# One pass over the weights for token groups 0 and 1, a sign taken as a bit, and batch 0's q and k transposed by TensorE

## The chip, the core and the metric

One core of one Trainium2 chip runs the whole kernel. The metric is the device time of one execution in microseconds (us). The kernel before was timed three times: 1012.99, 1014.65 and 1016.63 us, median 1014.65 us.

## The reference

Three layers run one after another, on 2304 tokens (4 batches of 576) of width 512 (8 heads of 64):

```python
scores = scale * q @ k.T + (cum[:, None] - cum[None, :])   # cum = cumsum(log f); causal mask
x = softmax(scores) @ v                                    # (4, 8, 576, 64) -> (2304, 512)
g = x @ w_gate;  x = silu(g) * (x @ w_val) @ w_out         # 512 -> 1536 -> 512, weights as float64
e = argmax(x @ r_gate);  gw = 1 / (sum(exp(l - max l)) + 1e-9)
out = gw * relu(x @ w1[e]) @ w2[e]                         # 8 experts, 512 -> 1024 -> 512
```

All three are computed to nearly float32, mostly by splitting each operand into a high and a low half (`hi`, `lo`) and adding three products: hi·hi, hi·lo and lo·hi.

## The kernel before, in words

**Attention.** Two heads make a pair `P`; batch 0 is pairs 0 to 3, and a batch has 16 steps ("slots"). In slot i, `part1` scores one item (a head and a half of its query blocks; L279), `part2` (L340) casts and splits the probabilities of item i-1 and has them transposed by a DMA (L366, `pt<-p`), and `pv` (L371) multiplies item i-2 by the values. While pair P runs, pair P+1 is prepared: `scales` (L191) finds a power of two for q and k, and `prep` (L216) splits q and k of one head into f16 halves side by side on the 128 partitions (L230 and L235 on ACT, L234 on DVE) and has them transposed by a DMA (L237, `qkt<-qks`). A score block is then two matmuls (L262, L263), one for the decay (L265) and one for the mask (L270).

**Weights.** The weights of the second layer arrive as 64-bit floats. `decode` (L871) rebuilds a 128x512 float32 tile from one 512 KB load of word pairs (`lo`, `hi`): two ACT operations on the high word (L878 the magnitude, L879 the sign as +1 or -1), a shift on DVE (L880), a shift-and-or on DVE that brings in the low word (L881), and a multiplication by the sign on POOL (L884). `w_split` (L900) then makes f16 halves of the gate and value weights (L909 on ACT, L910 on DVE), and `wo_dec` (L912) splits an output weight tile. For each j of 6 (256 of the 1536 inner columns) there are nine such tasks: 4 decodes and 2 splits of gate and value weights, one small one, and 2 output-weight decodes; over all j 36 decodes. The list `tasks` (L923) holds them in order of j. The load buffers are one tile and four not-yet-used weight tiles of j = 4 and 5; from j = 3 on fewer of these are left.

**Second layer.** Tokens go in 9 groups `g` of 256; a unit u is one (g, j): `unit_g` (L521) and `unit_v` (L532) are 24 matmuls each (L503), and `unit_o` (L546) adds 12 matmuls (L556) into two PSUM tiles `yp`, which stay open over the six j of a group. `fin0` (L587) copies them out and writes the rows to DRAM (`y_d`). Units run in the order u = 6g + j (L522).

**Order of the work.** The code is written as a list with due points, and a planner then places each engine's instructions by that order and by when operands should be ready. Before unit 0 come the first 18 slots, all of batch 0, and with them 43 of the 57 tasks (`PRE`, L1148, L1160), that is all of j = 0 to 3 and most of j = 4. The rest follow at the units that need them (`mark`, `markw`, L1109, L1174). Slots of batch 1 start to be dealt out after unit 4 and are due at unit 10 (`pts_`, L1165); group 2, which begins batch 1's tokens, is unit 12.

**Third layer.** `fin1`, `fin2` (L608, L638) find each token's expert and its gate weight `gw`, write the latter to DRAM (`g_d`, L735), and list tokens by expert. Experts follow one by one; a last tile of overflowing tokens gathers its gate weights from `g_d` (L1366), and a loop (L1414) is there for more such tiles.

Of the kernel before, what the change touches and what calls it, by code (L numbers as in the profile page):

```python
# [12 lines left out]
U32 = mybir.dt.uint32  # L13
# [14 lines left out]
def kernel(  # L28
# [37 lines left out]
    g_d = dram.tile([NT + 1, 1], F32, name="g_d")  # L66
# [19 lines left out]
    cnt = const.tile([128, NE], F32, name="cnt")  # L86
    sv = const.tile([128, 2, B], F32, name="sv")
# [9 lines left out]
    def consts():  # L97
# [32 lines left out]
        vec.memset(cnt, 0.0)  # L130

# [24 lines left out]
    qk_in = [ap_.tile([128, 2, NCH, D], F32, name=f"qk_in{i}") for i in range(NQK)]  # L156
# [34 lines left out]
    def scales(P):  # L191
        am = st_p.tile([128, 2], F32, tag="am", bufs=2, name="am")
        jk = qks_p.tile([128, 3 * NCH, 2, D], F16, tag="qks", name="jk").rearrange("p (a c) h d -> p a c h d", a=3)
        for a in range(2):
            act.activation(
                out=jk[:, a].rearrange("p c h d -> p h c d"), in_=qk_in[(2 * P + a) % NQK], func=ACTF.Square,
                accum_out=am[:, a:a + 1],
            )
# [16 lines left out]

    def prep(P, hh):  # L216
        sc, c = stt[P]
# [20 lines left out]
        heads[P, hh] = (qkt, c[1][:, hh, :])  # L238
# [19 lines left out]
    def score(ps, o, hd, j, k0, k1):  # L258
        qkt, pk = hd
        n = k1 - k0  # L260
        lq = qkt[:, 0, 128 * j:128 * j + 128]
        pe.matmul(out=ps[:, o:o + n], lhsT=lq, rhs=qkt[:, 1, k0:k1], start=True, stop=False, skip_group_check=True)  # L262
        pe.matmul(out=ps[:, o:o + n], lhsT=lq, rhs=qkt[:, 2, k0:k1], start=False, stop=False, skip_group_check=True)  # L263
# [256 lines left out]

    def unit_g(u):  # L521
        g, j = divmod(u, KF // 2)  # L522
# [9 lines left out]
    def unit_v(u, t):  # L532
        g, j = divmod(u, KF // 2)
# [12 lines left out]
    def unit_o(u):  # L546
        g, j = divmod(u, KF // 2)
        hi, lo = hbuf.pop(u)
        if j == 0:
            yps[g] = [ps_y.tile([128, DM], F32, tag=f"y{i}", name="yp") for i in range(2)]  # L550
        for i in range(2):
            n_ = 0
            for fi in range(2):
                fk = 2 * j + fi
                for hx, wx in ((hi, 0), (hi, 1), (lo, 0)):
# [4 lines left out]
                        start=(j == 0 and n_ == 0),  # L560
                        stop=(j == KF // 2 - 1 and n_ == 5),
# [24 lines left out]

    def fin0(g):  # L587
        ys = M["y"].tile([128, 2, DM], F32, tag="ys", name="ys")
        act.activation(out=ys[:, 0, :], in_=yps[g][0], func=ACTF.Copy)
        vec.tensor_copy(out=ys[:, 1, :], in_=yps[g][1])  # L590
# [47 lines left out]
    def fin2(g):  # L638
# [96 lines left out]
        rows_out(g_d, g, gw)  # L735
# [37 lines left out]
    def start():  # L773
# [25 lines left out]
        act.dma_start(out=g_d[NT:NT + 1, :], in_=zr[:, 0:1])  # L799
# [71 lines left out]
    def decode(src, n):  # L871
        c = c_tile()
        raw = fetch(src, n, c.rearrange("p (a n) -> p a n", a=n))
        if raw is not None:
# [3 lines left out]
            act.activation(out=c, in_=hi.bitcast(F32), func=ACTF.Abs, scale=2.0 ** -112)  # L878
            act.activation(out=hi.bitcast(F32), in_=hi, func=ACTF.Sign)  # L879
# [4 lines left out]
            gp.tensor_tensor(out=c, in0=c, in1=hi.bitcast(F32), op=ALU.mult)  # L884
# [37 lines left out]
    NJ = KF // 2  # L922
# [179 lines left out]
    def unit(u, between=None):  # L1102
# [5 lines left out]
        if u > 0:  # L1108
            if u - 1 < NJ:  # L1109
                upto(markw[u - 1])  # L1110
            unit_o(u - 1)
            g1, j1 = divmod(u - 1, NJ)
# [10 lines left out]
            if j1 == NJ - 1:  # L1123
                if g1 == 0:
                    sg.close()
                    M.update(routing_pools())
# [21 lines left out]
    PRE0, PRE = 2, 43  # L1148
# [16 lines left out]
    pts_ = [(-1, first), (NJ - 2, first), (2 * NJ - 2, 8 * NP + 2), (4 * NJ - 1, 12 * NP + 2), (6 * NJ - 2, NSL)]  # L1165
# [7 lines left out]
    for u in range(NU + 1):  # L1173
        if u < NJ:  # L1174
            upto(mark[u])
        if u < NU and u % NJ == 0:
            for b, _, _ in spans(min(u // NJ + 1, NG - 1)):
# [4 lines left out]
        if u < NU:  # L1182
            need = 4 * NP * ((G * (u // NJ + 1) - 1) // S + 1) + 2
        tgt = pace(u)
        slots(need)
        unit(u, lambda: slots(min(tgt, nslot[0] + 1)))
# [162 lines left out]

    def gate(s, t):  # L1350
# [4 lines left out]
    for s in range(NE + 1):  # L1355
        nxt = s + 1 if s < NE else None
        if s == 2:
# [8 lines left out]
            gp.indirect_dma_start(  # L1366
                out=gwo, out_offset=None, in_=g_d[:, :],
                in_offset=bass.IndirectOffsetOnAxis(ap=ixo.bitcast(U32), axis=0),
            )
# [19 lines left out]
        if nxt is not None:  # L1389
            if nxt == 1:  # L1390
                transp(xts[1], 0, xgs[1], bank)
            else:
                turn(xts[nxt % 2], xgs[nxt])
        if nxt == NE:
# [16 lines left out]
    with tc.tile_pool(name="lw", bufs=1) as lw, tc.tile_pool(name="lr", bufs=3) as lr, tc.tile_pool(  # L1411
        name="lx", bufs=1
    ) as lx, tc.tile_pool(name="lp", bufs=2, space=PSUM) as lp:
        with tc.For_i(1, n_ov) as it:  # L1414
# [8 lines left out]
            gp.indirect_dma_start(  # L1423
# [56 lines left out]
```

## Time and profile before

| | |
|---|---|
| median of 3 runs | 1014.65 us |
| the profiled execution's own time | 1012.41 us |
| its span, first to last instruction | 1010.6 us |
| busy: TensorE (PE) | 882.2 us, 87% |
| busy: VectorE (DVE) | 614.9 us, 61% |
| busy: ScalarE (ACT) | 555.3 us, 55% |
| busy: GpSimd (POOL) | 389.6 us, 39% |
| mean granted TensorE clock | 0.943 |

The shares are means over stages that differ. The page cuts the span into 40 slices of 25.3 us: in the first six or seven PE is half idle while DVE and ACT are nearly full, and later PE is busy at 95% or more. "Releaser" in a wait is what ended an engine's idle time. Clock 1.00 is 2.4 GHz and 0.50 is 1.2 GHz.

### The profile page before, as it was taken

Reading aid. Unit: us, or ns where it says so; the run is one execution under the profiler, and the core shown is the slowest. Engines: PE = TensorE matmul, PEld = TensorE weight load, DVE = VectorE, ACT = ScalarE, POOL = GpSimd, SP = SyncE. Lnnn points to the kernel's source line nnn. Section 1 sums busy time; section 2 is a strip of 40 time slices with the busy share of each in tenths; the row PEclk is TensorE's granted clock in tenths of the full one; section 3 lists DMA queues with packets and bytes.
Section 4 is the critical chain, followed back from the end, with each engine's and each line's share of the span. In section 5 each row is a group of like instructions: output and inputs, shape, how many; then the busy total and the mean of one; then the engine's idle time right before and its main releaser. Section 6 shows DMA issues by size and latency. Waiting matters only on the chain.

```text
span 1010.6 us, 19838 instructions
## 1 busy us (share of the span) xinstructions
PE 882.2 (87%) x7028; PEld 734.7 (73%) x7053; DVE 614.9 (61%) x1818; ACT 555.3 (55%) x1205; POOL 389.6 (39%) x467
## 2 busy tenths in 40 slices
PE   1545557998999989999999999898989999999995
PEld 0334336877777868888878888687869788889894
DVE  6999888487666746565644434334536675665540
ACT  5987988476677666665633322122425454555431
POOL 1468676464444425344442222222245632100101
PEclk9995657999999999999999999899989999999998
DMA  8897998347886787567545422112376887765420
GB/s 244 209 216 205 230 204 187 90 101 165 180 172 146 164 190 158 101 133 137 102 113 143 121 22 64 5 18 66 71 180 187 218 219 201 215 198 159 132 95 34
DMA packets 309481, 146.35 MB, mean 145 GB/s; under 512 B 273441, under 2 KB 285857, under 8 KB 309380
## 3 DMA queue, kind: packets, MB, share of 16 engines
q1 hardware_dynamic: 305088, 134.68, 56.2%
q0 software_dynamic: 4096, 10.24, 3.7%
q8 instruction: 56, 0.92, 0.4%
q14 instruction: 45, 0.37, 0.2%
q10 hardware_dynamic: 196, 0.14, 0.0%
HBM read 84.24 MB, written 10.31 MB: 94 GB/s over the span
## 4 chain that ended last, share of the span: by engine, by line
PE 46%; DMA 17%; issue 12%; DVE 6%; ACT 3%; SPq 2%; POOL 2%; POOLq 0%; DVEq 0%; ACTq 0%
PE yp L556 11%; PE g L503 10%; PE v L503 10%; DMA out_dram<-o,ix 5%; PE bank L1218 3%; DMA pt<-p 3%; PE px L387 2%; DMA pair<-yt 2%; PE bank L1261 2%; DMA pair<-words 2%; DMA wr<-in_moe_w_dram 1%; PE ps L262 1%; PE ps L263 1%; DVE wlo L978 1%; PE ps L265 1%
## 5 line engine op out<-in xcount | busy, mean ns | idle before, releaser
L352 POOL TENSOR_TENSOR p<-st,p 128x128 f16<-128x128 f32 (+3 forms) x128 | 110.1, 864 | 102.1 <-issue 62.7
L543 POOL TENSOR_TENSOR lo<-t,hi 128x512 fp32r<-128x512 f32 x54 | 70.1, 1299 | 149.3 <-ACT hi L542 121.6
L503 PE MATMUL g<-xr,wga 128*128 128x256 f16 x864 | 106.1, 277 | 0.3 <-DVE t L529 0.3
L503 PE MATMUL v<-xr,wva 128*128 128x256 f16 x864 | 106.2, 277 | 0.0
L327 ACT ACTIVATE st<-st,nb,c 128x64 f32<-128x64 f32 (+4 forms) x160 | 102.6, 643 | 0.9
L503 PEld LDWEIGHTS <-wga 128*128 128x128 f16 x864 | 82.6, 100 | 17.2 <-issue 6.6
L503 PEld LDWEIGHTS <-wva 128*128 128x128 f16 x864 | 84.8, 101 | 10.6 <-issue 0.3
L387 PE MATMUL px<-vs,pt 128*128 128x64 f16 x1280 | 56.3, 203 | 39.3 <-DMA pt<-p 28.8
L349 DVE CAST p<-st 128x64 f16<-128x64 f32 (+4 forms) x160 | 68.4, 442 | 31.6 <-ACT st L327 20.1
L317 DVE CUSTOM_DVE_ANT_0 st<-ps,zero 128x64 f32<-128x64 f32 (+3 forms) x160 | 55.8, 377 | 50.9 <-PE ps L270 48.8
L387 PEld LDWEIGHTS <-pt 128*128 128x128 f16 x1280 | 50.3, 105 | 49.3 <-DMA pt<-p 32.8
L363 POOL TENSOR_TENSOR p<-st,p 128x64 f16<-128x64 f32 (+1 forms) x128 | 54.1, 424 | 70.6 <-issue 36.4
L262 PE MATMUL ps<-qkt 128*128 128x64 f16 (+2 forms) x192 | 56.5, 312 | 21.1 <-DMA qkt<-qks 7.2
L526 ACT ACTIVATE t<-g,gscale 128x512 f32<-128x512 f32 (+3 forms) x72 | 39.4, 573 | 62.2 <-PE g L503 59.0
L1012 POOL DMA_INDIRECT out_dram<-o,ix x24 | 24.6, 1026 | 123.3 <-ACT o L1263 79.5
L542 ACT ACTIVATE hi<-t 128x512 fp32r<-128x512 f32 x54 | 33.8, 625 | 56.5 <-DVE t L536 56.5
L556 PE MATMUL yp<-wohi,hi 128*128 128x512 f32 x144 | 60.6, 421 | 0.0
L263 PE MATMUL ps<-qkt 128*128 128x64 f16 (+2 forms) x192 | 60.1, 315 | 0.0
L1223 ACT ACTIVATE h<-bank 128x320 fp32r<-128x320 f32 (+1 forms) x64 | 26.3, 422 | 60.1 <-PE bank L1218 59.8
L1225 DVE SCALAR_TENSOR_TENSOR h<-bank,h 128x64 fp32r<-128x64 f32 (+2 forms) x128 | 33.4, 305 | 40.4 <-ACT h L1223 40.4
L556 PE MATMUL yp<-wohi,lo 128*128 128x512 f32 x144 | 57.6, 402 | 0.0
L556 PE MATMUL yp<-wolo,hi 128*128 128x512 f32 x144 | 57.1, 397 | 0.0
(322 smaller groups left out, 2483.2 us busy)
## 6 DMA issues: line engine op xcount, KB each, us to landing
wr<-in_moe_w_dram SPq DMA_DIRECT2D x72, 512.0 KB, 5.1
vr<-in_v_dram SPq DMA_DIRECT2D x16, 288.0 KB, 4.5
qk_in<-in_q_dram SPq DMA_DIRECT2D x32, 128.0 KB, 2.5
qk_in<-in_k_dram SPq DMA_DIRECT2D x32, 128.0 KB, 2.6
v_in<-in_v_dram SPq DMA_DIRECT2D x32, 128.0 KB, 3.0
y_d<-ys SPq DMA_DIRECT2D x6, 512.0 KB, 3.5
wgb<-in_moe_w_gate_dram SPq DMA_DIRECT2D x5, 512.0 KB, 5.9
raw<-in_moe_w_val_dram SPq DMA_DIRECT2D x5, 512.0 KB, 4.2
```

Of the source, the lines that this page charges most:

```text
L262: pe.matmul(out=ps[:, o:o + n], lhsT=lq, rhs=qkt[:, 1, k0:k1], start=True, stop=False, skip_group_check=True)
L263: pe.matmul(out=ps[:, o:o + n], lhsT=lq, rhs=qkt[:, 2, k0:k1], start=False, stop=False, skip_group_check=True)
L317: vec.tensor_tensor_reduce(out=sts[m][:, k0 - 64:k1 - 64], in0=ps[:, o:o + n], in1=zero.to_broadcast([128, n]), scale=1.0, scalar=init, op ...
L327: act.activation(out=sts[m], in_=sts[m], func=ACTF.Exp, scale=c[:, 0:1], bias=nb[:, m:m + 1], accum_out=sm[:, m, hh:hh + 1],)
L349: vec.tensor_copy(out=flat[:, o + 64:o + 64 + n], in_=src)
L352: gp.tensor_tensor(out=flat[:, o1:o1 + n - 64], in0=src[:, 64:n], in1=flat[:, o + 128:o + 64 + n], op=ALU.subtract)
L363: gp.tensor_tensor(out=blk[:, :, 0:64], in0=pair, in1=blk[:, :, 64:128], op=ALU.subtract)
L387: pe.matmul(out=px[:, 128 * m + 64 * hh:128 * m + 64 * hh + 64], lhsT=pm[:, o + ph * last + c, :], rhs=vs[:, hh, c, vh, :], start=(c == 0 ...
L503: pe.matmul(out=ps[:, fi, :], lhsT=w16[:, kk, wi, 128 * fi:128 * fi + 128], rhs=xr[:, kk, x0:x0 + 2, xi, :], start=(n_ == 0), stop=(n_ == ...
L526: act.activation(out=t[:, :, c0:c1], in_=gps[:, :, c0:c1], func=ACTF.Tanh, scale=gscale[:, b, j:j + 1])
L543: last["lo"] = gp.tensor_tensor(out=lo, in0=t, in1=hi.bitcast(F32), op=ALU.subtract)
L556: pe.matmul(out=yps[g][i], lhsT=hx[:, fi, 128 * i:128 * i + 128], rhs=wo[fk][wx], start=(j == 0 and n_ == 0), stop=(j == KF // 2 - 1 and n ...
```

## The change

- **Order.** Units run as (0,0) (0,1) (0,2), then group 1's six, then (0,3) (0,4) (0,5), then groups 2 to 8. So j = 3, 4, 5 are first needed at units 6, 7, 8. Group 0's half sum is copied out of PSUM and written to `y_d` (`part_out`), and `fin0(0)` reads it back and adds the second half.
- **Tasks.** 27 of the 57 (j = 0 to 2) are traced with batch 0's slots; the other 30 with units 0 to 4. Slots of batch 1 are dealt out from unit 0 on and are due at unit 10 as before.
- **Decode.** The magnitude keeps nothing of the sign; a second shift-and-or form on DVE takes the sign bit from the high word. L879 (ACT) and L884 (POOL) go.
- **Batch 0's q and k** (`prep0`): ten TensorE transposes of 128x128 per pair into PSUM, both heads at once; ACT and DVE then scale, split and write f16 halves, q once per head with the other head's rows multiplied by 0. A score block has three products instead of two. L230, L234, L235 and L237 are not run for these pairs; batches 1 to 3 keep them.
- **Gate weights** are no longer written to DRAM; the overflow tile computes its own (`gate_of`: 8 small matmuls and five short operations).

The core of the diff:

```diff
+    def prep0(P):
+        vec.tensor_scalar(out=qm, in0=half, scalar1=sc[:, 0, 0:1], scalar2=None, op0=ALU.mult)
...
+        for a in range(2):
+            src = qk_in[(2 * P + a) % NQK]
...
+            for x in range(NCH):
+                o = ps[:, 128 * x:128 * x + 128] if x < NCH - 1 else last_[:, 128 * a:128 * a + 128]
+                pe.transpose(out=o, in_=src[:, :, x, :], identity=ident)
...
+            for n0, n1, p in parts:
+                if a == 0:
+                    for h in range(2):
+                        act.activation(out=two[h][:, 0, n0:n1], in_=p, func=ACTF.Copy, scale=qm[:, h:h + 1])
+                        vec.scalar_tensor_tensor(
+                            out=two[h][:, 1, n0:n1], in0=p, scalar=qm[:, h:h + 1], in1=two[h][:, 0, n0:n1],
+                            op0=ALU.mult, op1=ALU.subtract,
+                        )
+                else:
+                    s1 = sc[:, 0, 1:2]
+                    act.activation(out=two[0][:, 2, n0:n1], in_=p, func=ACTF.Copy, scale=s1)
+                    vec.scalar_tensor_tensor(
+                        out=two[1][:, 2, n0:n1], in0=p, scalar=s1, in1=two[0][:, 2, n0:n1], op0=ALU.mult,
+                        op1=ALU.subtract,
+                    )
...
+            heads[P, h] = ([(qh, kh), (ql, kh), (qh, kl)], c[1][:, h, :])
...
+    CUT = 3
+    order = (
+        [(0, j) for j in range(CUT)] + [(1, j) for j in range(NJ)] + [(0, j) for j in range(CUT, NJ)]
+        + [(g, j) for g in range(2, NG) for j in range(NJ)]
+    )
...
+    def part_out():
+        r = [c_p.tile([128, DM], F32, tag="c", name="yc") for _ in range(2)]
+        act.activation(out=r[0], in_=yps[0][0], func=ACTF.Copy)
+        vec.tensor_copy(out=r[1], in_=yps[0][1])
+        for i in range(2):
+            sp.dma_start(out=y_d[r0_of(i):r0_of(i) + 128, :], in_=r[i])
...
     def fin0(g):
         ys = M["y"].tile([128, 2, DM], F32, tag="ys", name="ys")
+        if g == 0:
+            rows_out(y_d, g, ys, True)
+            for i in range(2):
+                vec.tensor_tensor(out=ys[:, i, :], in0=ys[:, i, :], in1=yps[g][i], op=ALU.add)
...
-            act.activation(out=c, in_=hi.bitcast(F32), func=ACTF.Abs, scale=2.0 ** -112)
-            act.activation(out=hi.bitcast(F32), in_=hi, func=ACTF.Sign)
+            act.activation(out=c, in_=hi.bitcast(F32), func=ACTF.Copy, scale=2.0 ** -112)
...
-            gp.tensor_tensor(out=c, in0=c, in1=hi.bitcast(F32), op=ALU.mult)
+            vec.scalar_tensor_tensor(
+                out=ci, in0=hi, scalar=-2 ** 31, in1=ci, op0=ALU.bitwise_and, op1=ALU.bitwise_or
+            )
...
-    PRE0, PRE = 2, 43
+    PRE0, PRE = 2, 27
...
-    pts_ = [(-1, first), (NJ - 2, first), (2 * NJ - 2, 8 * NP + 2), (4 * NJ - 1, 12 * NP + 2), (6 * NJ - 2, NSL)]
+    pts_ = [(-1, first), (2 * NJ - 2, 8 * NP + 2), (4 * NJ - 1, 12 * NP + 2), (6 * NJ - 2, NSL)]
...
+        if u < 2 * NJ:
+            upto(27 + (len(tasks) - 27) * (u + 1) // 5)
...
+    def gate_of(xt, ps, pool, dst):
+        p = ps("t")[:, 0:NE]
+        prods = [(x, kk) for kk in range(KD) for x in xt]
+        for n_, (x, kk) in enumerate(prods):
+            pe.matmul(
+                out=p, lhsT=x[:, kk, 0:128].bitcast(F32), rhs=rg[:, kk, 0:NE], start=(n_ == 0),
+                stop=(n_ == len(prods) - 1), skip_group_check=True,
+            )
...
```

## Rows read from the trace of the kernel before

**Rows 1.** The page's 40 slices: busy tenths of DVE, granted clock in tenths.

```profile
DVE  6999888487666746565644434334536675665540
PEclk9995657999999999999999999899989999999998
```

**Rows 2.** Stretches of the span, all engines: busy us (instructions), granted clock, DMA share, GB/s.

```profile
core 0: us, PE busy (x) PEld busy (x) DVE busy (x) ACT busy (x) POOL busy (x), PEclk, DMA share, GB/s
0.00:25.00 25.00, 2.93 (x10) 2.50 (x10) 15.80 (x55) 14.88 (x33) 4.46 (x15) 1.00 0.86 244
25.00:165.00 140.00, 76.54 (x623) 54.44 (x629) 127.99 (x360) 124.12 (x308) 90.17 (x99) 0.71 0.90 212
165.00:312.00 147.00, 137.11 (x1336) 111.49 (x1341) 102.93 (x304) 102.23 (x254) 75.06 (x96) 0.99 0.65 145
```

**Rows 3.** PE in order of time: first scores, eight fp32 matmuls, group 2's first unit.

```profile
26.71 0.23 PE L262 MATMUL ps<-qkt 128*128 128x64 f16 x1 [3.91 <-DMA qkt<-qks]
...
202.41 0.95 PE L805 MATMUL tot<-totw,onesf 128*128 128x1 f32 x8
...
312.18 2.78 PE L503 MATMUL g<-xr,wga 128*128 128x256 f16 x24
```

**Rows 4.** Who PE waited for from 165 to 312 us: us in total, times, longest.

```profile
PE px L387 <- DMA pt<-p: 6.1, 6, 1.5
...
PE ps L262 <- DMA qkt<-qks: 1.5, 2, 1.0
```

**Rows 5.** Line L881 alone (DVE): sum to 312 us, then shortest/median/longest ns.

```profile
sum 312.00, DVE 30.20; mean DVE 10.07
...
L881 DVE SCALAR_TENSOR_TENSOR c<-raw,c x10: 674/693/1656, 14.9 to 217.3; 128x512 int32<-128x512 int32 x10
```

**Rows 6.** Line L880 alone (DVE), in the same form.

```profile
sum 312.00, DVE 22.00; mean DVE 7.33
...
L880 DVE TENSOR_SCALAR c<-c x19: 408/427/1519, 14.4 to 215.4; 128x512 int32<-128x512 int32 x19
```

**Rows 7.** Line L349 alone (DVE): two stretches.

```profile
25.00:165.00 140.00, 22.97 (x43) 0.71 0.90 212
165.00:312.00 147.00, 17.86 (x43) 0.99 0.65 145
```

**Rows 8.** Line L884 alone (POOL): two stretches, and the sum to 312.

```profile
0.00:25.00 25.00, 2.58 (x2) 1.00 0.86 244
25.00:165.00 140.00, 35.92 (x25) 0.71 0.90 212
sum 312.00, POOL 50.56; mean POOL 16.85
```

**Rows 9.** DVE groups to 312 us by shape: busy, mean ns, idle before.

```profile
L234 DVE SCALAR_TENSOR_TENSOR qks<-qk_in,sc,qks 128x320 f16<-128x320 f32 x40 | 23.0, 607 | 0.5 <-ACT qks L230 0.5
...
L529 DVE SCALAR_TENSOR_TENSOR t<-t,g 128x512 f32<-128x512 f32 x13 | 8.8, 680 | 5.2 <-ACT t L526 5.1
...
L317 DVE CUSTOM_DVE_ANT_0 st<-ps,zero 128x64 f32<-128x64 f32 x36 | 7.7, 215 | 2.9 <-PE ps L270 2.5 <-POOL p L363 0.3
L317 DVE CUSTOM_DVE_ANT_0 st<-ps,zero 128x192 f32<-128x192 f32 x18 | 6.3, 349 | 0.0
```

**Rows 10.** 25 to 165 us: L910 alone (DVE), then L262 and L429 (PE, PEld).

```profile
25.00:165.00 140.00, 15.47 (x18) 0.71 0.90 212
...
25.00:165.00 140.00, 20.36 (x54) 8.66 (x54) 0.71 0.90 212
...
25.00:165.00 140.00, 5.26 (x18) 2.73 (x18) 0.71 0.90 212
```

**Rows 11.** DMA to 165 us: the main queue (packets, MB, share) and one issue; then `y_d`.

```profile
q1 hardware_dynamic: 83820, 35.53, 88.7%
...
qkt<-qks SPq DMA_TRANSPOSE x10, 4.6
...
y_d<-ys SPq DMA_DIRECT2D x6, 512.0 KB, 3.5
```

More of the change, by code (lines that the diff above doesn't have):

```diff
@@ L86 @@
     cnt = const.tile([128, NE], F32, name="cnt")
+    half = const.tile([128, 2], F32, name="half")
     sv = const.tile([128, 2, B], F32, name="sv")
@@ L130, in consts @@
         vec.memset(cnt, 0.0)
+        vec.memset(half, 0.0)
+        vec.memset(half[0:64, 0:1], 1.0)
+        vec.memset(half[64:128, 1:2], 1.0)
     wo_p = ctx.enter_context(tc.tile_pool(name="wo", bufs=1, side="right"))
@@ L155 @@
     NQK, NV, NPB, NBLK = 3, 1, 4, 9
-    qk_in = [ap_.tile([128, 2, NCH, D], F32, name=f"qk_in{i}") for i in range(NQK)]
+    qk_in = [
+        ap_.tile([128, NCH, 2, D], F32, name=f"qk_in{i}").rearrange("p c h d -> p h c d") for i in range(NQK)
+    ]
     v_in = [ap_.tile([128, 2, NCH, D], F32, name=f"v_in{i}") for i in range(NV)]
@@ L258, in score @@
     def score(ps, o, hd, j, k0, k1):
-        qkt, pk = hd
+        prods, pk = hd
         n = k1 - k0
-        lq = qkt[:, 0, 128 * j:128 * j + 128]
-        pe.matmul(out=ps[:, o:o + n], lhsT=lq, rhs=qkt[:, 1, k0:k1], start=True, stop=False, skip_group_check=True)
-        pe.matmul(out=ps[:, o:o + n], lhsT=lq, rhs=qkt[:, 2, k0:k1], start=False, stop=False, skip_group_check=True)
+        for x, (lq, rk_) in enumerate(prods):
+            pe.matmul(
+                out=ps[:, o:o + n], lhsT=lq[:, 128 * j:128 * j + 128], rhs=rk_[:, k0:k1], start=(x == 0), stop=False,
+                skip_group_check=True,
+            )
         d0 = max(k0, 128 * j)
@@ L532, in unit_v @@
     def unit_v(u, t):
-        g, j = divmod(u, KF // 2)
+        g, j = order[u]
         vps = gv(g, j, 1, "v")
@@ L559, in unit_o @@
                         rhs=wo[fk][wx],
-                        start=(j == 0 and n_ == 0),
-                        stop=(j == KF // 2 - 1 and n_ == 5),
+                        start=(j in opens and n_ == 0),
+                        stop=(j in shuts and n_ == 5),
                     )
@@ L1108, in unit @@
         if u > 0:
-            if u - 1 < NJ:
-                upto(markw[u - 1])
+            g1, j1 = order[u - 1]
+            if g1 < 2:
+                upto(markw[j1])
             unit_o(u - 1)
-            g1, j1 = divmod(u - 1, NJ)
+            if (g1, j1) == (0, CUT - 1):
+                part_out()
             if g1 == NG - 1 and j1 < len(EP["w2"]):
@@ L1173 @@
     for u in range(NU + 1):
[L1174 to L1177, printed above, removed]
+        g, j = order[min(u, NU - 1)]
+        if u < 2 * NJ:
+            upto(mark[j])
+        if u < NU and (u == 2 * NJ - 1 or u % NJ == 0 and u >= 2 * NJ):
+            for b, _, _ in spans(min((u + 1) // NJ + (u % NJ == 0), NG - 1)):
                 if b not in unscaled:
@@ L1393 @@
                 turn(xts[nxt % 2], xgs[nxt])
+                if nxt == NE:
+                    gate_of(xts[nxt % 2], bank, ix_p, gwo)
         if nxt == NE:
@@ L1445 @@
             transp(xt, 0, xs, lbank)
+            gate_of(xt, lbank, lx, gwl)
             hh, hl = [lx.tile([128, KF2, 128], F32R, name=f"lh{x}") for x in ("h", "l")]
```

70 lines of the change are left out of this document (48 added, 22 removed).

## The prediction

> **What bounds the kernel now.** I read the 40 slices first, then the time in stretches, then who PE waited for, and last single lines. The slices show DVE full and PE's granted clock at half while batch 0 and the first weights are done, and the opposite later [rows 1]. The stretches give it in numbers [rows 2]. From 25 to 165 us DVE is busy 127.99 of 140 us (91%), ACT 124.12 (89%), the DMA engines 90%, and PE only 76.54 at a mean clock of 0.71: PE waits, and three others are near full at once. From 165 to 312 us PE is busy 137.11 of 147 (93%) at clock 0.99, and DVE 102.93 (70%). 312 us is where group 2 begins [rows 3]; by then batch 1's attention, all 36 decodes and the twelve units of groups 0 and 1 are done, and both kernels must have done the same work there. Past it nothing but the overflow tile's gate weights is changed, so I count **only the time until group 2 begins**, and add the other 698.4 us of the span as they are.
>
> In the second stretch PE waits 6.1 us for transposed probabilities and 1.5 for transposed q and k [rows 4], and no weight task is among its waits there. So needing j = 3 to 5 three units later relieves no wait of the old kernel. It only allows 16 tasks to leave the first stretch. The gain has to come from there, and what is moved has to be paid on the same DVE beside PE.
>
> **The change part by part, on DVE until group 2.** Before: 15.80 + 127.99 + 102.93 = 246.7 us [rows 2]. Moving tasks changes nothing in this sum.
>
> The sign: 36 instructions of the form of L881. These took 30.20 us for 36, a mean of 0.84, and the shortest 0.674 [rows 5]. So +24.3 to +30.2; I take 0.75 each, between the two, since POOL will be less busy: **+27.0**.
>
> Batch 0's q and k: per pair three 512-wide and three 128-wide instructions on PSUM and one tiny one. L529 does 512 from PSUM in 0.68; 64 and 192 columns take 0.215 and 0.349, so 128 some 0.28 [rows 9]; with 0.15 for the tiny one 3.0 us per pair, 12.1 for four. Away go 16 of L234 at 23.0/40 = 0.575, 9.2 us [rows 9]. **+2.9**; bounds 0 and +6.
>
> Relief: POOL loses 36 multiplications, 50.56 us, of which 2.58 + 35.92 = 38.5 by 165 us, where POOL is busy 94.6 in all [rows 2, 8]. DVE instructions were longer while POOL was busy: L880 22.00 - 36 x 0.408 = 7.3 us over its shortest [rows 6], L881 30.20 - 36 x 0.674 = 5.9 [rows 5], and L349 0.534 each in the first stretch against 0.415 in the second, 5.1 us for 43 [rows 7]: 18.3 together. The multiplications are 41% of POOL's time there, which gives 7.5; other lines suffer too, so I take **-10**; bounds 0 and -40 (36 times 1.519 - 0.408, the longest L880 over the shortest).
>
> The Trainium skill (SBUF — State Buffer, Who interferes with whom) says that a VectorE instruction with two SBUF inputs contends with a GpSimd instruction that reads SBUF, and that the loser waits for the other's whole instruction. The longest L880 and L881, 1.1 and 1.0 us over their shortest, agree. The rule also speaks against the change: the sign instruction has two SBUF inputs and stays exposed to POOL's probability splits; at 0.84 us each the sum would be 3.2 us more.
>
> Sum until group 2: 246.7 + 27.0 + 2.9 - 10 = **266.6 us**. DVE was busy 79% of the 312 us; it now has to be busy 85% only to come out even.
>
> First stretch. DVE had done 143.8 us by 165. Away: 11 decodes (29 were done, 18 are needed) at 0.611 + 0.839 = 1.45, 16.0; 6 of L910 at 15.47/18 = 0.86, 5.2 [rows 5, 6, 10]. Added: 18 signs, 13.5, and 2.9; relief -8 of the 10. 131.0 us are left. The start: the first scores stand at 26.71 behind a DMA transpose [rows 3] which lands 4.6 us after its issue [rows 11]; ten PE transposes are quicker, and I take 5 us (bounds 0 and 10, the idle 9.2 us of DVE in the first 25). At the old rate of 0.914 the rest, 115.2 us, takes 126. Batch 0 ends at 25 - 5 + 126 = **146 us** instead of 165.
>
> The others follow. ACT loses the signs, 16 tasks and the old q and k, more than it gains. DMA: 35.53 MB took 88.7% of 165 us, 4.1 us per MB [rows 11]; eight transposes of 0.49 MB and eleven loads of 0.52 MB are 40 us less of 147. PE gains 48 third products at 20.36/54 = 0.38 and 40 transposes at 5.26/18 = 0.29 [rows 10], 30 us on 79.5, and is still 75% busy of 146 at half clock. SP loses eight transposes. All that lies under DVE.
>
> Second stretch. DVE has 266.6 - 131.0 = 135.6 us, PE its 137 as before, which took 147. PE's pace would need DVE at 92%, above what it reached when PE waited for it. In return ACT and DMA are further from full than when it ran at 91%. I take 0.90: 150.7 us. Group 2 begins at **297 us**, 15.5 earlier.
>
> Edits with small prices. `part_out` copies two banks at unit 3; behind it waits `unit_o(3)`, which comes after unit 4's 48 matmuls, 5.6 us at 2.78 for 24 [rows 3]: covered, but for a late c tile up to 5 us. `fin0(0)` reads rows back (a write of `y_d` takes 3.5 [rows 11]) and adds twice 0.7: 5 us, again under the next unit's matmuls, exposed up to 5 us if not. `gate_of`: 8 small fp32 matmuls like the eight in 0.95 us [rows 3]: **+1 us** on PE near the end, its chain of short operations beside the last expert's products. The 14 small writes of `g_d`, their issues on SP and POOL's gather go; nothing waited for them: 0.
>
> The profiled execution took 1012.4 us itself (span 1010.6): 1012.4 - 15.5 + 1 = 997.9. The median of the runs is 2.2 above that execution, so 1000.
>
> **The rivals.** (a) *The lock was the larger cost.* If each multiplication held one DVE instruction for most of its time, as that rule would have it, 27 us come back instead of 10, and if the start saves 10 us, batch 0 is done at 15 + (114 - 15.8)/0.914 = 122, and PE's 147 us from there end at 269 to 273: 39 us earlier, 977. For it: 1.5 us instances of L880. Against: the mean excess of the rows is half a microsecond per multiplication.
>
> (b) *The first stretch is a chain, not work.* If batch 0's slots go from score to exponent to transpose to product at their own pace, taking work away shortens only the start: 160 us, and then 151: 311, a us earlier than before and one paid for the gate, 1014.6. The three engines at 89 to 91% speak against it [rows 2]. This is also the case in which the shared pass doesn't do what it is for, since no weight wait is there to be removed.
>
> (c) *Slower: DVE becomes the bound beside PE.* Place: units 0 to 11, where 18 decodes, 16 slots and the units' own two DVE instructions queue on one engine in a fixed order. PE stands behind a score's maximum or a late weight tile. DVE's rate there was 0.70; 166 us until 312 make 135.6/166 = 0.82 the point below which the time is lost. At 0.78 the stretch takes 174 and ends at 320: 8 later and 1 for the gate, 1024. For it: in no long stretch were PE and DVE both above 90%. Against: the twelve units are 720 matmuls or more, at 2.78/24 each [rows 3] over 80 us for PE in hand, that need little of DVE.
>
> **How the numbers follow.** Forecast 0.62 (rates from 0.83 to 0.95), (a) 0.13, (b) 0.12, (c) 0.13. A measurement can tell about 0.3%, 3 us. Faster is the forecast and (a), 0.75; same (b), 0.12; slower (c), 0.13. The range takes the forecast's rates, the unknown relief and most of (a) and (c): 979 to 1021; what lies outside is the strong half of (a) and of (c).
>
> **What would show it.** Right: group 2's first matmul near 297, batch 0's last product near 150, DVE above 85% in both stretches, POOL's busy time down by about 50 us, L880 and L349 shorter on the mean, PE's waits after batch 0 not much above the old 9. Wrong: first stretch unchanged with DVE idle in it (b); PE's waits for DVE or weights after 150 us beyond 20 us (c); L880 near its 0.41 everywhere and group 2 before 280 (a). A change past group 2 of more than 3 us would show that I cut the kernel at the wrong place.

## The result, and the profile after

The changed kernel takes **989.8 us** (median of 4 runs, 988.34 to 992.02) against 1015.64 for the kernel before (4 runs, 1012.99 to 1018.56): ratio 0.9747, interval 0.9713 to 0.9781, 25.8 us faster. The forecast was 1000 with a range of 979 to 1021. The profiled execution took 989.82 us, its span is 988.0, against 1012.41 and 1010.6 before: 22.6 us of span are to be found.

The 40 slices and the stretches of the kernel after, which answer to [rows 1] and [rows 2]; the columns are those of [rows 2]:

```profile
DVE  7999997978757457466553544435546776566540
PEclk9875777999999999999999999999999999999998
```

```profile
30.00:60.00 30.00, 18.20 (x134) 11.18 (x134) 30.00 (x92) 24.82 (x65) 13.01 (x15) 0.83 0.83 207
60.00:90.00 30.00, 18.18 (x154) 12.12 (x151) 30.00 (x80) 22.09 (x58) 18.01 (x22) 0.56 0.96 207
90.00:120.00 30.00, 19.45 (x167) 13.69 (x168) 30.00 (x88) 25.09 (x67) 12.52 (x17) 0.67 0.87 200
...
sum 312.00, PE 231.51 PEld 177.16 DVE 263.86 ACT 229.49 POOL 135.45; mean PE 115.75 PEld 88.58 DVE 131.93 ACT 114.74 POOL 67.73
```

DVE, not 91% busy any more, is busy without a gap from 30 to 120 us, and at 139.5 us it makes batch 0's last cast of probabilities. The last line is the sum from the start to 312 us: DVE 263.86, PE 231.51. 312 us is where group 2 began before, and it is where it begins now. One correction to the record belongs here: the row at 312.18 in [rows 3] is group 2's second unit. A row of the kernel before at 307.30 (`L503 MATMUL g<-xr,wga`, 15 of its 24 matmuls in the records) is the first; its v step stands on DVE at 312.7, and at 311.7 in the kernel after. I use that v step as the mark from here on.

So where do 22.6 us come from? I took marks in each trace from the times of single instructions: batch 0's last cast of probabilities on DVE (the 40th of 160 casts), the end of its last product on PE, group 2's first v step, the casts done by then, the last unit's v step, and the end.

```
                 batch 0's  batch 0's     group 2's  casts by  group 2 to  last unit  span
                 last cast  last product  first v    then      last unit   to end
before           156.9      166.0         312.7      87        414.7       283.1      1010.6
after            139.5      159.3         311.7      93        396.2       280.1       988.0
difference       -17.4       -6.7          -1.0      +6        -18.5        -3.0       -22.6
```

The last products themselves, first before, then after, and the stretches up to them and on to group 2's first v step, before and after:

```profile
165.43 0.59 PE L387 MATMUL px<-vs,pt 128*128 128x64 f16 x14
158.74 0.58 PE L440 MATMUL px<-vs,pt 128*128 128x64 f16 x14 [1.98 <-DMA pt<-p]
```

```profile
0.00:166.00 166.00, 80.47 (x651) 57.93 (x657) 144.44 (x414) 140.00 (x341) 95.64 (x115) 0.75 0.89 217
166.00:312.70 146.70, 136.81 (x1325) 111.12 (x1329) 102.97 (x308) 101.93 (x253) 74.06 (x95) 0.99 0.65 146
0.00:159.30 159.30, 92.98 (x771) 65.27 (x772) 151.15 (x461) 126.69 (x320) 68.06 (x94) 0.76 0.89 204
159.30:311.70 152.40, 138.23 (x1336) 111.67 (x1333) 112.41 (x332) 102.50 (x252) 67.09 (x89) 0.94 0.78 158
```

DVE's part of batch 0 is done 17.4 us earlier, but the last product comes only 6.7 us earlier, and the stretch behind it is 5.7 us longer (152.4 against 146.7). In that stretch PE is busy 138.23 us (91%, mean clock 0.94) and DVE 112.41 (74%).

One microsecond comes before group 2, three after the last unit, and 18.5 between, where the prediction changed nothing. Two things are to be seen there. **First, PE's waits** from 312 to 560 us, before and after (columns: us in total, times, longest):

```profile
PE px L387 <- DMA pt<-p: 3.9, 3, 1.8
PE g L503 <- DVE t L529: 0.3, 1, 0.3
```

```profile
PE g L556 <- DVE t L589: 0.2, 1, 0.2
```

The waits for transposed probabilities are gone. Six more casts were done when group 2 began: attention stood further ahead. **Second, the routing of a group.** In order of time on SP, ACT, DVE and PE, first before, then after (in square brackets the idle time ahead of an instruction and what ended it):

```profile
624.69 1.74 SPq L571 DMA_DIRECT2D g_d<-gw  x3
626.55 1.28 SPq L620 DMA_TRANSPOSE pair<-yt  x1
...
635.84 0.77 ACT L622 ACTIVATE yt<-pair 128x512 uint16<-128x512 uint16 x1 [9.12 <-DMA pair<-yt]
635.85 0.45 DVE L623 COPY yt<-pair 128x512 uint16<-128x512 uint16 x1 [6.86 <-DMA pair<-yt]
636.98 0.20 DVE L736 TENSOR_TENSOR rb<-eq,gw 128x48 f32<-128x48 f32 x1
637.23 1.09 PE L716 MATMUL rk<-rb,ra 128*128 128x48 f32 x4 [4.72 <-DVE rb L736]
```

```profile
617.93 1.23 SPq L697 DMA_TRANSPOSE pair<-yt  x1
...
621.09 0.46 DVE L700 COPY yt<-pair 128x512 uint16<-128x512 uint16 x1 [2.19 <-POOL lo L603]
...
625.07 0.54 PE L793 MATMUL rk<-rb,ra 128*128 128x48 f32 x4
```

Before, three small writes of gate weights stand just ahead of a transpose on SP's queue. The transpose is issued at 626.55 and its data are there at 635.84, 9.3 us later. DVE stands behind the copy that needs it, its short routing operations stand behind that copy, and PE behind one of them, for 4.72 us. PE's clock then is low as well; the stretch right behind it, in the kernel before:

```profile
636.00:643.00 7.00, 5.77 (x20) 4.62 (x21) 2.82 (x11) 1.78 (x3) 2.19 (x2) 0.54 0.00 0
```

For the last 5.3 us of the 9.3 the core's DMA engines move nothing (the last two columns), so it is not their load that the transpose waits for then:

```profile
630.50:635.80 5.30, 2.01 (x19) 1.55 (x16) 0.00 (x0) 0.00 (x0) 0.00 (x0) 1.00 0.00 0
```

After, the writes are gone, the transpose issued at 617.93 is copied at 621.09, 3.2 us later, and PE does not wait. Over the routing stretch from 560 us, before (to 732) and after (to 715), DVE's and PE's waits for this are:

```profile
DVE yt L623 <- DMA pair<-yt: 16.7, 5, 6.9
...
PE rk L716 <- DVE rb L736: 7.3, 2, 4.7
```

```profile
DVE yt L700 <- DMA pair<-yt: 6.0, 3, 3.0
```

### The profile page after: what moved, and what is told of

It reads as the page before. It is cut to its first block, busy times and chain, and to the rows that moved or that the text cites. A ratio compares the mean times of both kernels' runs of the same rounds, so it can differ in the third digit from the quotient of the medians.

```text
span 988.0 us, 19993 instructions
## 1 busy us (share of the span) xinstructions
PE 889.9 (90%) x7157; PEld 739.8 (75%) x7157; DVE 629.4 (64%) x1876; ACT 538.4 (54%) x1170; POOL 350.1 (35%) x430
## 4 chain that ended last, share of the span: by engine, by line
PE 63%; DMA 12%; DVE 12%; issue 6%; ACT 2%; POOL 2%; SPq 2%; POOLq 0%; DVEq 0%; ACTq 0%
PE yp L618 13%; PE g L556 12%; PE v L556 12%; PE bank L1341 8%; PE bank L1298 8%; PE ps L313 3%; PE px L440 2%; DMA pt<-p 2%; DMA out_dram<-o,ix 2%; DMA qkt<-qks 2%; DMA pair<-words 2%; DVE st L370 1%; PE ps L318 1%; DVE p L402 1%; DVE wo L955 1%
## 5 line engine op out<-in xcount | busy, mean ns | idle before, releaser
L405 POOL TENSOR_TENSOR p<-st,p 128x128 f16<-128x128 f32 (+3 forms) x128 | 114.1, 894 | 146.2 <-issue 94.3
L416 POOL TENSOR_TENSOR p<-st,p 128x64 f16<-128x64 f32 (+1 forms) x128 | 60.0, 469 | 111.1 <-issue 53.6
L402 DVE CAST p<-st 128x64 f16<-128x64 f32 (+4 forms) x160 | 64.4, 409 | 34.5 <-ACT st L380 32.5
L313 PE MATMUL ps<-qkt 128*128 128x64 f16 (+4 forms) x288 | 53.4, 287 | 15.3 <-DMA qkt<-qks 13.7
L440 PE MATMUL px<-vs,pt 128*128 128x64 f16 x1280 | 54.0, 201 | 14.3 <-DMA pt<-p 12.9
L318 PE MATMUL ps<-cum,nc 128*128 128x64 bf16 (+2 forms) x192 | 57.3, 304 | 0.0
```

What stands on the lines that cost most here:

```text
L313: pe.matmul(out=ps[:, o:o + n], lhsT=lq[:, 128 * j:128 * j + 128], rhs=rk_[:, k0:k1], start=(x == 0), stop=False, skip_group_check=True,)
L318: pe.matmul(out=ps[:, o:o + n], lhsT=pk, rhs=cum3[:, k0 - 64:k1 - 64], start=False, stop=(k1 <= d0), skip_group_check=True,)
L402: vec.tensor_copy(out=flat[:, o + 64:o + 64 + n], in_=src)
L405: gp.tensor_tensor(out=flat[:, o1:o1 + n - 64], in0=src[:, 64:n], in1=flat[:, o + 128:o + 64 + n], op=ALU.subtract)
L440: pe.matmul(out=px[:, 128 * m + 64 * hh:128 * m + 64 * hh + 64], lhsT=pm[:, o + ph * last + c, :], rhs=vs[:, hh, c, vh, :], start=(c == 0 ...
```

## The experiments

The change has four parts: **gate** (no gate weights in DRAM), **order** (the shared pass with `part_out`, the 27 tasks and the new due points), **sign** (the bit on DVE), **prep** (batch 0's q and k by TensorE). I tried each alone on the kernel before, and each taken out of the kernel after; then four kernels for what that left open.

**Gate alone, and all but gate.** The edit of the first, and the reverse of it for the second:

```diff
-    g_d = dram.tile([NT + 1, 1], F32, name="g_d")
...
-        rows_out(g_d, g, gw)
...
-        act.dma_start(out=g_d[NT:NT + 1, :], in_=zr[:, 0:1])
...
+    def gate_of(xt, ps, pool, dst):
...
-            gp.indirect_dma_start(
-                out=gwo, out_offset=None, in_=g_d[:, :],
-                in_offset=bass.IndirectOffsetOnAxis(ap=ixo.bitcast(U32), axis=0),
-            )
...
+                if nxt == NE:
+                    gate_of(xts[nxt % 2], bank, ix_p, gwo)
```

> The kernel before with one part of the change alone: gate weights are not written to DRAM, the overflow tile computes its own. Theory A (the 14 small writes of the gate weights stand in SP's queue ahead of the transposes of the routing stretch and delay them): 13 us faster, about 1003 us, PE's waits for rb gone, the transposes of yt land in about 3 us each time. Theory B (the prediction: nothing waited for these writes): 1016 us, within 3 us.

> The changed kernel with that one part taken back: gate weights written to DRAM and gathered again. Theory A: 13 us slower than the changed kernel, about 1003 us, with single transposes of yt that take 6 to 9 us to land again. Theory B: 990 us, within 3 us.

Measured: alone 1004.05 us, ratio 0.9900 (0.9868 to 0.9931); without it 1010.41, ratio 0.9965 (0.9938 to 0.9991). DVE's wait for the transposes from 540 to 740 us, gate alone, then all but gate:

```profile
DVE yt L622 <- DMA pair<-yt: 10.3, 5, 2.9
```

```profile
DVE yt L701 <- DMA pair<-yt: 14.6, 3, 7.0
```

The longest wait is 2.9 us without the writes and 7.0 with them. PE's waits for `rb`, the routing operation above, are gone in the first and 7.2 us in the second. Alone, the part leaves group 2's first v step where it was (312.9 against 312.7) and shortens the way from there to the last unit by 10.5 us (404.2 against 414.7): all of its gain, and all of it in the place that the prediction costed at nothing. That is theory A's place and cause, with some 10 us for its 13. Taken back, the part costs 20.6 us; some 9 us lie on this way (405.3 against 396.2), and the rest before group 2 and behind the last unit, where placement scatters, as shown below.

**Order alone, and all but order.** The core of the first edit; the second takes the same lines out of the kernel after, and so has 43 tasks beside batch 0 again:

```diff
+    order = (
+        [(0, j) for j in range(CUT)] + [(1, j) for j in range(NJ)] + [(0, j) for j in range(CUT, NJ)]
+        + [(g, j) for g in range(2, NG) for j in range(NJ)]
+    )
...
-    PRE0, PRE = 2, 43
+    PRE0, PRE = 2, 27
...
+            upto(27 + (len(tasks) - 27) * (u + 1) // 5)
```

> The kernel before with the shared pass alone: units of groups 0 and 1 interleaved, 27 tasks with batch 0 and 30 with units 0 to 4; signs, q and k, gate weights as before. Theory A (the step of the prediction: DVE loses some 21 us of work in the first stretch and gets the same work back beside PE, which has slack): batch 0's last product 20 us earlier, 8 to 14 us faster, about 1005 us. Theory B (DVE becomes the bound beside PE, with POOL's multiplications still there): batch 0 earlier but group 2 not, 1013 to 1020 us.

> The changed kernel with the old order of units and 43 tasks beside batch 0. Theory A (the shared pass carries the part of the gain before group 2): about 1002 us. Theory B (sign and q and k carry it, the order is worth little): 988 to 993 us.

Measured: alone 1025.96, ratio 1.0134 (1.0079 to 1.0188), slower; without it 1017.82, ratio 1.0034 (1.0010 to 1.0057). Order alone, to batch 0's last product and on to group 2, and the largest waits around batch 0's last items (147 to 195 us):

```profile
0.00:185.30 185.30, 87.29 (x724) 61.79 (x730) 156.00 (x456) 155.64 (x384) 102.35 (x122) 0.71 0.85 206
185.30:328.00 142.70, 129.96 (x1281) 107.43 (x1287) 101.83 (x284) 93.15 (x227) 79.56 (x97) 0.96 0.79 156
```

```profile
POOL p L352 <- DVE p L349: 14.7, 2, 10.1
DVE p L349 <- DMA pt<-p: 6.5, 4, 2.2
PE px L387 <- DVE mx L317: 5.6, 1, 5.6
```

DVE makes batch 0's last cast at 154.5, 2.4 us earlier than before, and its last product comes at 185.3, 19 us later than before. The stretch behind it is 4 us shorter (142.7 against 146.7), so group 2 begins 15 us late. By the last product 29 of the 36 decodes are done, as many as before: tasks that leave the list beside batch 0 do not thereby leave the stretch. Theory B has group 2 right; neither has the last product or the time. Taken out of the kernel after, the part costs more than either theory there says. From group 2 to the last unit it is 5.8 us quicker than before (408.9 against 414.7), with 93 casts done at its begin against 87.

**Sign alone, and all but sign.**

```diff
-            act.activation(out=c, in_=hi.bitcast(F32), func=ACTF.Abs, scale=2.0 ** -112)
-            act.activation(out=hi.bitcast(F32), in_=hi, func=ACTF.Sign)
+            act.activation(out=c, in_=hi.bitcast(F32), func=ACTF.Copy, scale=2.0 ** -112)
...
-            gp.tensor_tensor(out=c, in0=c, in1=hi.bitcast(F32), op=ALU.mult)
+            vec.scalar_tensor_tensor(
+                out=ci, in0=hi, scalar=-2 ** 31, in1=ci, op0=ALU.bitwise_and, op1=ALU.bitwise_or
+            )
```

> The kernel before with the sign taken as a bit alone: 36 instructions more on DVE, 36 fewer on ACT and 36 fewer on POOL. Theory A (the prediction's ledger: 27 us more on DVE, 10 us back because POOL blocks it less): batch 0 about 12 us later and the whole 5 to 15 us slower, 1020 to 1030 us. Theory B (POOL's multiplications held DVE for longer than the ledger says, or POOL was itself in the chain): 1000 to 1012 us.

> The changed kernel with the sign multiplied in on POOL again. Theory A: 5 to 15 us faster than the changed kernel, 975 to 985 us. Theory B: 994 to 1005 us.

Measured: alone 1016.32, ratio 1.0011 (0.9991 to 1.0031), no difference; without it 1006.22, ratio 0.9912 (0.9892 to 0.9931). Sign alone:

```profile
0.00:160.40 160.40, 76.14 (x661) 55.92 (x667) 141.08 (x431) 123.87 (x307) 64.19 (x89) 0.72 0.94 217
160.40:315.50 155.10, 139.45 (x1307) 111.36 (x1310) 110.94 (x322) 97.91 (x243) 61.75 (x80) 0.97 0.65 146
sum 315.50, PE 215.59 PEld 167.28 DVE 252.03 ACT 221.78 POOL 125.94; mean PE 107.80 PEld 83.64 DVE 126.01 ACT 110.89 POOL 62.97
```

With 43 tasks still beside it, batch 0's last cast comes at 145.5 (156.9 before) and its last product at 160.4 (166.0), and group 2 begins 3 us later. DVE has 36 more instructions and its sum to group 2 is 252.0, against 246.7 [rows 2]: 5 us more, not 27. The time lies between the two theories, and taken out, the part makes the kernel slower, about as theory B there has it.

**Prep alone, and all but prep.** The whole of `prep0` as in the diff above; the kernels differ in

```diff
+        if P < NP:
+            if hh == 0:
+                prep0(P)
+            return
```

> The kernel before with batch 0's q and k transposed by TensorE alone. Theory A (DVE bounds the first stretch, only the start is shorter and the DMA less full): 3 to 8 us faster, 1008 to 1012 us. Theory B (the first stretch waits for transposes by DMA): 12 us or more faster, below 1004 us. Third: PE at half clock becomes the bound with 30 us more work, 1016 us or slower.

> The changed kernel with batch 0's q and k split and transposed by DMA again. Theory A: 3 to 8 us slower than the changed kernel, 993 to 998 us. Theory B: 12 us or more slower, above 1001 us. Third: 990 us or faster.

Measured: alone 1039.69, ratio 1.0224 (1.0169 to 1.0279), much slower; without it 989.52, ratio 0.9751 (0.9725 to 0.9776), the changed kernel's own time. Prep alone, then all but prep, to batch 0's last product and on to group 2:

```profile
0.00:184.10 184.10, 96.87 (x752) 70.30 (x759) 153.07 (x446) 147.65 (x361) 105.25 (x126) 0.69 0.74 181
184.10:331.70 147.60, 134.15 (x1292) 108.79 (x1297) 89.82 (x289) 93.26 (x228) 63.11 (x83) 0.99 0.69 134
```

```profile
0.00:156.50 156.50, 78.45 (x678) 57.20 (x683) 134.75 (x414) 119.06 (x301) 64.83 (x92) 0.73 0.91 217
156.50:306.90 150.40, 137.42 (x1331) 112.10 (x1338) 126.12 (x364) 110.24 (x273) 72.58 (x92) 0.95 0.77 170
```

Alone, the transposes take the DMA engines from 89% to 74%, and batch 0's last product comes 18 us later (184.1 against 166.0): emptier DMA engines did not shorten this stretch. PE is busy 231 us to group 2, against 217 before [rows 2], and batch 0 is the place where it runs at about 0.7 of its clock; by its time this is the third case of the expectation, but PE is busy only 96.87 of the 184.1 us, so that PE is the bound is not shown. In the changed kernel the part is worth nothing, again the third case: without it batch 0's last product comes 2.8 us earlier (156.5) and group 2 5 us earlier (306.9), and the way on to the last unit is 4 us longer.

**Gate weights written from another queue.** The gate part is taken back, and only these writes go by ACT's queue, so that no transpose stands behind them on SP's:

```diff
-            sp.dma_start(out=s_ if back else d, in_=d if back else s_)
+            (act if dst is g_d else sp).dma_start(out=s_ if back else d, in_=d if back else s_)
```

> The changed kernel with the gate weights written to DRAM and gathered again, but the writes issued from ACT's queue, not from SP's in front of the transposes. Theory A (order on SP's queue is what delays the transposes): the stretch from batch 3's last product to the last unit takes 182 us as in the changed kernel, and no transpose of yt lands later than 4 us. Theory B (the writes slow the transposes from any queue, or the planner keeps the two apart): that stretch takes 191 us, as with the writes on SP.

Measured: 1022.19, ratio 1.0072 (1.0044 to 1.0100). ACT's queue and SP's, and the wait, in this kernel:

```profile
633.32 1.83 ACTq L634 DMA_DIRECT2D g_d<-gw  x3
...
633.71 1.24 SPq L698 DMA_TRANSPOSE pair<-yt  x1
```

```profile
DVE yt L701 <- DMA pair<-yt: 24.7, 3, 9.6
```

The transpose issued at 633.71 is copied at 640.98, 7.3 us later, with the writes on another queue, and the longest wait is 9.6 us. It is not the order on one queue. From batch 3's last product on PE to the last unit it takes 194.1 us, against 182.4 with the writes on SP and 173.2 without them (the expectation's 191 and 182 start at an ACT operation 8.4 us ahead of that product). Group 2 to the last unit takes 417.0 us, the second longest of all kernels.

**A change that should change nothing.** The kernel after, with one 4-byte write to an unused DRAM tile at the start:

```diff
+    g_d = dram.tile([NT + 1, 1], F32, name="g_d")
...
+        act.dma_start(out=g_d[NT:NT + 1, :], in_=zr[:, 0:1])
```

> The changed kernel with one 4-byte write to DRAM more, at the start, and nothing else: it does no work. Theory A (the planner places everything anew for the smallest change, and the times up to group 2 scatter by some 7 us for that alone): group 2 begins at 316 to 322 us, or before 306, and the whole lies 5 to 10 us off the changed kernel's. Theory B (the placement is stable): group 2 at 312, 990 us within 3.

Measured: 997.22, ratio 0.9838 (0.9803 to 0.9874): 7.4 us over the changed kernel and clear of its interval, for a write that nothing reads. The planner has placed the work anew: DVE's instructions in the two traces come in the same order for the first 12.5 us, and the next is an operation of q and k in the one (12.56 us) and one of a decode in the other (15.43 us). To the last product of batch 0, and on to group 2:

```profile
0.00:172.70 172.70, 100.08 (x797) 70.67 (x805) 160.17 (x503) 136.08 (x350) 67.95 (x97) 0.73 0.83 199
172.70:316.30 143.60, 130.98 (x1296) 108.11 (x1301) 100.21 (x289) 91.16 (x224) 65.03 (x87) 0.98 0.77 155
```

The same work, no more of it on any engine, stands in another order: batch 0's last product comes 13.4 us later (172.7 against 159.3), group 2 begins 4.6 us later, and another 3 us are lost behind the last unit. From group 2 to the last unit the two agree within 0.2 us (396.4 and 396.2). So a difference of some 8 us between two kernels here, and of some 13 at batch 0's last product, can be placement alone, and what is told of single parts before group 2 holds only where it is larger.

**43 tasks beside batch 0 in the changed kernel.**

```diff
-    PRE0, PRE = 2, 27
+    PRE0, PRE = 2, 43
```

> The changed kernel with 43 tasks beside batch 0 instead of 27, the order of units and the dealing out of slots as changed. Theory A (moving the 16 tasks is what the shared pass is good for): 1000 to 1010 us, batch 0's last product near 156. Theory B (the even dealing out of batch 1's slots from unit 0 is): 988 to 994 us, with group 2 at 312 in spite of a later batch 0.

Measured: 1002.58, ratio 0.9890 (0.9855 to 0.9926), 13 us over the changed kernel. Batch 0's last product comes at 177.3 instead of 159.3, and group 2 begins at 318.8 instead of 311.7. Against the kernel with the needless write these are 4.6 and 2.5 us, and 5 us of the whole, which placement could make. By the last product 31 decodes are done instead of 29: with the new order the 16 tasks are no longer listed beside batch 0, and most of them still run there. By its time this is theory A; that the moved tasks are the reason is not shown. (The expectation's 156 is again an ACT operation's time, 24 us ahead of the last product here.)

**A slower pace for the moved tasks.** On the kernel without prep, the last 30 tasks go with units 0 to 7:

```diff
-            upto(27 + (len(tasks) - 27) * (u + 1) // 5)
+            upto(27 + (len(tasks) - 27) * (u + 1) // 8)
```

> The changed kernel without batch 0's transposes by TensorE, and with the last 30 tasks spread over units 0 to 7 instead of 0 to 4. Theory A (right after batch 0 DVE is full, 98% from 129 to 200 us, and has room later): group 2 at 298 to 303, 980 to 986 us. Theory B (the weights of j = 3 to 5 then come late for units 6 to 8): 992 us or more.

Measured: 993.94, ratio 0.9806 (0.9775 to 0.9836), against 989.52 for the kernel it is made from. Batch 0's last product is at 154.7 and 156.5, group 2's first v step at 306.9 in both. The pace does not set it.

All marks together, worked out from the traces as above (`cast` and `product` are batch 0's last ones, `decodes` how many of the 36 were begun by that product):

```
                 batch 0:               group 2's  casts by  group 2 to  gate weights  order
                 cast  product  decodes first v    then      last unit   written
before           156.9 166.0    29      312.7      87        414.7       yes           old
sign alone       145.5 160.4    27      315.5      85        415.3       yes           old
prep alone       163.5 184.1    31      331.7      87        421.8       yes           old
order alone      154.5 185.3    29      328.0      93        408.9       yes           new
all but gate     145.2 174.8    29      319.2      93        405.3       yes           new
by ACT's queue   145.5 175.3    29      319.6      93        417.0       yes           new
gate alone       156.7 171.6    30      312.9      87        404.2       no            old
all but order    157.0 175.5    31      327.2      88        405.3       no            old
after            139.5 159.3    29      311.7      93        396.2       no            new
needless write   144.3 172.7    29      316.3      93        396.4       no            new
all but sign     152.2 182.5    29      325.8      93        396.5       no            new
43 tasks         153.8 177.3    31      318.8      93        398.0       no            new
units 0 to 7     126.4 154.7    23      306.9      93        399.8       no            new
all but prep     126.9 156.5    23      306.9      93        400.1       no            new
```

The way from group 2 to the last unit sorts by two things alone, whatever came before: 414.7 to 421.8 with neither part, 404.2 and 405.3 with gate, 405.3 to 408.9 with order (417.0 where ACT's queue writes), 396.2 to 400.1 with both. Gate is worth 9 to 11 us there, order 6 to 9. Batch 3's last product cuts this way in two, and each half sorts by one part: up to it 229.0 to 235.8 us in the old order and 222.8 to 226.2 in the new, from it on 182.4 to 186.0 with the writes (194.1 by ACT's queue) and 173.2 to 174.9 without. In the six kernels that write, PE waits 6.5 to 12.7 us for `rb`; in the eight that do not, at most 0.5.

## Why the prediction was right, and where it was not

The sign and the range were right, and that was mostly luck: of the 15.5 us forecast before group 2 one came, and 21.5 us came behind it, where the sum had nothing but one us the other way.

**The first stretch: the step that failed.** "Batch 0 ends at 146 us instead of 165": its last product came at 159.3 instead of 166.0, 6.7 us earlier and not 19. Two things in the working of this step did not hold. First, the work: 11 decodes were to leave the stretch, and none did. 29 of the 36 had been begun by the last product in both kernels, and DVE had worked 151.2 us by then and not 131.0. The list has 18 decodes beside batch 0; the planner placed those of the first units there as well. Second, a wait that the sum does not have. DVE's last cast of batch 0 came 17.4 us earlier, at 139.5, but from there to the last product it took 19.8 us instead of 9.2. The first is the stretch, the second and third are PE's waits in it:

```profile
139.50:159.30 19.80, 12.85 (x124) 10.24 (x123) 18.86 (x61) 15.87 (x42) 10.15 (x13) 0.74 0.98 185
...
PE ps L313 <- DMA qkt<-qks: 5.0, 1, 5.0
PE px L440 <- DMA pt<-p: 2.0, 1, 2.0
```

PE works 12.85 us of it at a clock of 0.74, and waits for a DMA transpose of batch 1's q and k, whose scores stand ahead in its order, and then for batch 0's own probabilities; the DMA engines are at 98%. In the kernels with the new order the way from the last cast to the last product is 19.8 to 30.9 us, in those with the old one 9.2 to 20.5. Why the new order draws it out was not tried. The rate was too low besides: I took 0.914, and DVE ran at 1.00 from 30 to 120 us and at 0.95 over the whole stretch. The start gained more than its 5 us: the first score stands at 17.84 instead of 26.71. Rival (b) gave the marks that were measured, 160, then 151, and 311 (159.3, 152.4 and 311.7). Its reason is not shown by that: DVE was not idle, and the work that it assumes to be taken away was still there.

**The ledger: right sum, wrong terms.** 266.6 us of DVE until group 2 forecast, 263.86 measured to 312, with six more casts done. The sign cost what was said. Its line, then the successors of [rows 5] and [rows 6], each alone to 312 us in the kernel after, 36 instructions each:

```profile
sum 312.00, DVE 27.41; mean DVE 13.71
...
sum 312.00, DVE 29.12; mean DVE 14.56
...
sum 312.00, DVE 19.56; mean DVE 9.78
```

That is 0.76 us a sign (forecast 0.75); L881's successor went from 30.20 to 29.12 and L880's from 22.00 to 19.56. But with sign alone DVE's whole sum rose by 5 us and not by 27, so the relief is about 20 us rather than 10 (two casts fewer were done by then), spread over many lines, and nearer to rival (a)'s 27 than to mine. L880 alone took 17.11 us there instead of 22.00, and the casts (L349) 33.88 for 85 instead of 40.83 for 86. ACT lost 36 operations in that kernel too, and the two were not tried apart. Prep alone took 4 us off DVE's sum (242.9) where I had added 2.9. The Trainium skill (SBUF — State Buffer, Who interferes with whom) has a VectorE instruction with two SBUF inputs and a GpSimd instruction that reads SBUF exclude each other; that agrees in direction, and the row above shows that the sign itself escaped most of it. L880 and the casts have one input each, so the sentence that the prediction rests on does not cover L880's long instances, which it counts as agreement. In the changed kernel the larger relief was used up by something that I had called nothing: "Moving tasks changes nothing in this sum". With the new order 93 casts are done at group 2's begin, and 87 before. The cut is not at the same work.

**The second stretch: near the number, for another reason.** I took DVE at 0.90 beside PE, 150.7 us. From the last product to group 2 it took 152.4, but DVE was busy 112.41 us of it (74%) and not 135.6, since 29 decodes lay behind it, and PE 138.23 (91%) for the 137 forecast. So PE set this stretch, with 14.1 us of waits in it (9.5 before), 11.0 of them for transposes by DMA:

```profile
PE px L440 <- DMA pt<-p: 7.9, 5, 3.1
PE ps L313 <- DMA qkt<-qks: 3.1, 1, 3.1
```

The sentence "it now has to be busy 85% only to come out even" was the exact one: 263.86 of 312 is 85%, and it came out even. Rival (c), DVE as the bound beside PE, would have shown as over 20 us of waits for DVE or weights; these waits are 3.1 us. Whether DVE's order or the fuller DMA engines (0.78 against 0.65) made the transposes late was not tried.

**"The other 698.4 us of the span as they are": failed, by 21.5 us.** Two terms of the sum were missing. For `g_d`, "nothing waited for them: 0" was 10 us. No wait names the writes, and that is why I missed them: a transpose that was issued behind them landed 6 us late, DVE waited for the transpose, PE for DVE, and PE's clock was 0.54 in the 7 us behind that. Both halves of the test and all fourteen kernels sort by it. For the order, 6 to 9 us, all of them up to batch 3's last product: this fits the six casts' worth of attention already done. Attention's four lines on PE from 140 to 312 us took 70.5 us for 53 casts, in the kernel after:

```profile
140.00:312.00 172.00, 23.26 (x120) 9.50 (x120) 0.92 0.80 161
140.00:312.00 172.00, 17.31 (x60) 6.23 (x60) 0.92 0.80 161
140.00:312.00 172.00, 12.31 (x60) 6.24 (x60) 0.92 0.80 161
140.00:312.00 172.00, 17.64 (x425) 15.40 (x425) 0.92 0.80 161
```

That is 1.33 us each, and by this estimate 8 us for six. So of the 15.5 us forecast before group 2 some 9 were gained, most of it as work done ahead, and 10 came from the gate weights; that this credit is the whole of the order's share was not tried by itself. Three us behind the last unit are left: the kernels spread from 278 to 286 there, and the needless write alone takes them back, so I put them down to placement.

**The parts do not add.** Alone they come to -1.0, +1.3, +0.1 and +2.2%, 2.7% slower together; all four are 2.5% faster. Order needs sign: order alone begins group 2 at 328.0, and with sign and gate (all but prep) at 306.9, while gate moves that mark by 0.2. The rows that go with it are POOL's 102.35 us busy up to batch 0's last product against 64.83. The 15 us that order alone loses before group 2 and the 19 us that prep alone loses lie before batch 0's last product (185.3 and 184.1, against 166.0). Why they are lost there, and why prep costs nothing in the whole change, is not settled; PE's extra work is in both (231 us to group 2, against 217), and the needless write alone moves this mark by 13.

No kernel that I ran is clearly faster than the changed one. All but prep is its equal with some 40 lines less.

## What to carry to other kernels

A transfer that nothing waits for can still be the cause of a wait: look at what was issued beside it and how long that took to land, against the same transfer elsewhere. A cut in time compares two kernels only if the same work lies on each side, so count that work (here the casts and the decodes) in both. A stage ends with the last instruction of its chain and not with that of the busiest engine: here DVE's last cast and PE's last product lie 9 to 31 us apart. And before single parts are given credit, run a change that ought to change nothing: where a planner places the instructions, its scatter (here 7 us of 990, and 13 at a mark inside) is the bound on what a difference of two kernels can say.

## What was not expected of the hardware

- A DMA transpose of the routing took 3.1 us to land when it was alone and 9.3 us with three writes of 1 KB in all, in 4-byte rows, issued 2 us ahead of it; with these writes on another engine's queue it was late as well (7.3 us). In the last 5.3 us of the 9.3 the core's DMA engines moved nothing. What holds it up then was not tried.
- DVE can be busy for 90 us without a gap beside an ACT at 80% and DMA at 89% (mean of the three rows from 30 to 120 us), so 0.91 was what its waits left, not a ceiling.
- With 36 multiplications less on POOL (and 36 operations less on ACT), DVE's other work was some 20 us shorter: about 0.6 us for each, of the 1.4 that one multiplication took [rows 8].
